# Attention first, then an ffn with seven of eight quarter products in both matmuls

## The chip, the cores and the metric

The kernel runs on one core of one Trainium2 chip. The core has a matrix engine (TensorE, PE in the profile, with its weight loads as PEld), a vector engine (VectorE, DVE), an activation engine (ScalarE, ACT), GpSimd (POOL), a queue engine that issues most DMAs (SyncE, SP), an on-chip memory of 128 partitions (SBUF), and eight accumulator banks for the matrix engine's results (PSUM). The metric is device time in microseconds (us), of which lower is better. All data is float32 unless said otherwise.

## The reference

Routed attention over 4 batches, 8 heads, 768 positions and head size 64, and on its output, as 3072 tokens of 512 features, a two-matmul ffn with 2048 hidden features.

```python
q_assign = argmax(q_n @ c_n.T)          # 16 centroids of each head; k_assign likewise
mask     = q_assign[..., :, None] == k_assign[..., None, :]
scores   = where(mask, (q @ k.T) / sqrt(D), -1e9)
attn     = exp(scores - max(scores));  attn /= sum(attn) + 1e-9
x        = (attn @ v).transpose(0, 2, 1, 3).reshape(3072, 512)
h        = x @ w_in                      # 512 x 2048
g        = h * erf(softplus(h))
out      = g @ w_out                     # 2048 x 512
```

The weights arrive as 64-bit floats and are turned into float32 on the chip.

## The kernel before, in words

**Attention.** Two heads of a batch form a pair; there are 16 pairs, four to a batch. `route` transposes q and k of a pair on DVE, multiplies them with the centroids on PE (`psim`), finds each position's best centroid, and writes it as extra rows of small bfloat16 tiles (`qm`, `km` in the trace). `shift` multiplies those tiles on PE (`sm`) and takes maxima on DVE (`nmx`), which give a shift for each query; `turn` transposes the shifts, and six row DMAs put them back into `qm`. A unit is one block of 128 keys against half of the queries (384) of a pair: `scores` makes four f32 matmuls' worth of `sc` and two bfloat16 ones, and ACT takes the exponential (`pr`). `accumulate` adds the exponentials on POOL (`acc`), `attend` multiplies them with v on PE (`av`), and after the sixth key block `divide` sums over partitions on PE (`psum`), forms the reciprocal on ACT and DVE, and writes the attention output to tiles `xT`, transposed, features on partitions. There are 12 units to a pair, 192 in all.

**Weights.** `fetch` brings a 512-wide piece of a weight as 64-bit words; `convert` turns it into float32 with three passes on ACT, two on DVE and one on POOL. There are 32 such steps.

**The ffn.** A chunk is `TB` = 256 tokens; there are 12. `hidden` makes, for each of the 16 blocks of 128 hidden features, four matmuls of 256 columns over the 512 input features, and DVE copies two blocks at a time from PSUM to `g`. `gate` runs softplus and erf on ACT and leaves the products with `h` to POOL. `project` makes, for each 128 tokens, 16 matmuls of 512 columns. For the last four chunks `project_fast` uses a form with seven products of quarter size in place of eight: its factors are sums of quarters of `g` and of `w_out`, made by DVE and POOL.

**Order.** The first four pairs (batch 0) run in "slots", one unit each: `plan` lists how many steps of `route` and `shift`, of this pair and of the next, and how many conversion steps go into each slot. The class `InOrder` pins every engine's instructions in the written order until `FIRST`. From then on attention of batches 1 to 3 goes two units at a time, and between the units a generator of ffn matmuls, `ffn_stream`, is drawn on by `pump` for as many cycles as keep the ffn in step. The ffn of batch 3 (three chunks) comes last and alone. So the ffn of a batch runs beside the attention of the next one.

A block of ffn work in the present form, the two lines that the change replaces:

```python
te.matmul(hp[:, a], lhsT=w_in[:, r, f0 : f0 + P], rhs=xTs[b * HP + r][c], ...)      # 768 of these
te.matmul(po, lhsT=gs[n][:, ft, tt * P : (tt + 1) * P], rhs=w_out[:, ft], ...)      # 8 chunks x 2 x 16
```

Nearly all instructions are recorded through line 61, the wrapper's call, so they are told apart by the names of their tiles.

Of the kernel before, what the change touches and what calls it, by code (L numbers as in the profile page):

```python
# [9 lines left out]
F32 = mybir.dt.float32  # L10
# [9 lines left out]
P = 128  # L20
# [11 lines left out]
GW = 2  # L32
TB = 256
NCHUNK = B * S // TB
# [3 lines left out]
OUT_AT = (4, 5, 6, 7, 4, 5, 6, 7, 5, 6, 7, 8, 7, 8, 8, 8)  # L38
# [5 lines left out]
XBUFS = (5, 6, 6)  # L44
SLOTS = 5


ASIDE = (*range(5), 6, *range(8, 8 + 2 * NJ), 10 + 2 * NJ, 12 + 2 * NJ)
REST = 4
FIRST = 2 * NJ * HP - 3  # L50
# [19 lines left out]
def kernel(  # L70
# [21 lines left out]
    stage = pool("stage", 1)  # L92
    vp = pool("vp", 2)
    rowp = pool("rowp", 2)
    routep = pool("routep", 1)
    small = pool("small", 2)
    accp = pool("accp", 2)
    xTp = pool("xTp", 1)
    actp = pool("actp", 2)
    gp = pool("gp", 2)  # L100
    outp = pool("outp", 1)
    ps_s = pool("ps_s", 2, space=PSUM)
    ps_x = pool("ps_x", 4, space=PSUM)

# [3 lines left out]
    rank = const.tile([P, C], F32, name="rank")  # L108
# [3 lines left out]
    w_in = const.tile([P, DM // P, DFF], F32, name="w_in")  # L112
    w_out = const.tile([P, NFT, DM], F32, name="w_out")
# [77 lines left out]
    n_w_in = len(w_steps)  # L191
    for f in range(NFT):
        w_steps.append((w_out[:, f], moe_w_out[f * P : (f + 1) * P]))


    places = [n % 8 for n in range(n_w_in)] + list(OUT_AT)
    converted = [0]

    def half_tile():
        return actp.tile([P, NFT // 2, TB], F32, name="a_s")  # L200

    steps = {}
    cut = []

    def fetch(done):

        for n in range(max(done + 1, 0), min(done + 5, len(w_steps))):
            at = places[n]
            if n in steps or (at < 8 and at in places[done + 1 : n]) or (at == 8 and n > done + 2):
                continue  # L210
            t = half_tile() if at == 8 else w_out[:, 2 * at : 2 * (at + 1)]
            t = t.rearrange("p f t -> p (f t)")[:, 0 : 2 * LC]
            nc.sync.dma_start(out=t.bitcast(U32), in_=w_steps[n][1])
            words = t.rearrange("p (n w) -> p n w", w=2)
            steps[n] = words[:, :, 1], words[:, :, 0], t.bitcast(I16)[:, 1 : 4 * LC : 4]

    def split(upto):

        for n in range(len(cut), upto + 1):
            if n not in steps:  # L220
                return
            cut.append(n)
            hi, lo, _ = steps[n]
            ae.activation(out=w_steps[n][0], in_=hi, func=ACT.Abs, scale=UP)
            ae.activation(out=lo.bitcast(I32), in_=lo.bitcast(U32), func=ACT.Copy, scale=2.0**-29)

    def signs(n):

        hi, _, upper = steps[n]

        ae.activation(out=upper, in_=hi, func=ACT.Prelu, scale=2.0**-25, alpha=2.0**90)

    def convert():

        for n in range(len(w_steps)):
            split(n)
            _, lo, _ = steps[n]
            w = w_steps[n][0]
            ve.tensor_scalar(out=w, in0=w, scalar1=2.0, scalar2=None, op0=ALU.max)
            signs(n)  # L240
            split(n + 1)

            fetch(n - 2 if n < n_w_in else n - 1)
            yield
            ve.tensor_scalar(
                out=w.bitcast(U32), in0=w.bitcast(U32), scalar1=3, scalar2=None, op0=ALU.logical_shift_left
            )

            ge.tensor_tensor(out=w.bitcast(I32), in0=w.bitcast(I32), in1=lo.bitcast(I32), op=ALU.add)
            converted[0] = n + 1  # L250
            yield

    load_qk(0)
    fetch(-1)
# [39 lines left out]
    def route(p):  # L294
# [37 lines left out]
        yield from (choose if p <= HP else choose_later)(p, sim, mx, hot, hotT, low, vectors)  # L332

    def choose(p, sim, mx, hot, hotT, low, vectors):
# [35 lines left out]
    def choose_later(p, sim, mx, hot, hotT, low, vectors):  # L370
        n = HW // C
        ve.tensor_tensor(
            out=sim, in0=sim, in1=mx.unsqueeze(2).to_broadcast([P, n, C]), op=ALU.is_equal
        )
        yield
        vectors("k")
        yield

        ve.tensor_tensor(
            out=sim, in0=sim, in1=rank.unsqueeze(1).to_broadcast([P, n, C]), op=ALU.mult  # L380
        )
        ve.reduce_max(out=mx, in_=sim, axis=AX.X)

        for r, op in ((slice(0, D), ALU.is_equal), (slice(D, P), ALU.subtract)):
            ve.tensor_tensor(
                out=hot[r].rearrange("p (g c) -> p g c", c=C), in0=sim[r],
                in1=mx[r].unsqueeze(2).to_broadcast([D, n, C]), op=op,
            )
        ve.transpose(out=hotT, in_=hot)
        yield  # L390
        for half in range(2):
            cols = slice(half * HW, (half + 1) * HW)
            for e in range(2):
                r = slice(e * D, e * D + Q)
                g = slice(half * Q, (half + 1) * Q)
                ve.tensor_scalar_mul(out=low["q"][r, e, cols], in0=hotT[g], scalar1=own[g, e : e + 1])
                g = slice(D + half * Q, D + (half + 1) * Q)
                ae.copy(out=low["k"][r, e, cols], in_=hotT[g])
        yield

    def shift(p):
# [5 lines left out]
        for h in range(2):  # L409
# [17 lines left out]
            if p >= HP:  # L427
                yield
                turn(p, h)
# [32 lines left out]
    xTs = {}  # L462
    done = set()
# [33 lines left out]
    def accumulate(u):  # L497
# [4 lines left out]
        if j == 1:  # L502
            st["acc", half] = accp.tile([P, 2, HW], F32, name="acc")
# [18 lines left out]
    def divide(u):  # L522
# [22 lines left out]
        x = xTs.setdefault(p, {})  # L545
        lo = half * HW
        while lo < (half + 1) * HW:
            c = lo // TB
            hi = min((c + 1) * TB, (half + 1) * HW)
            if c not in x:  # L550
                x[c] = xTp.tile([P, TB], F32, name=f"xT{c}", bufs=XBUFS[c])
            mine = slice(lo - half * HW, hi - half * HW)
            ve.scalar_tensor_tensor(
                out=x[c][:, lo - c * TB : hi - c * TB], in0=av[:, mine], scalar=av[:, HW : HW + 1],
                in1=den[:, mine], op0=ALU.add, op1=ALU.mult,
            )
            lo = hi
        done.add((p, half))
# [5 lines left out]
    TJ = TB // P  # L564
    CPB = S // TB

    def gate(n):

        h = gs[n]
        half = NFT // 2  # L570
        s = [half_tile() for _ in range(2)]
        for i in range(2):
            ae.activation(out=s[i], in_=h[:, i * half : (i + 1) * half], func=ACT.Softplus)
        for i in range(2):
            ae.activation(out=s[i], in_=s[i], func=ACT.Erf)

        for i in range(0, NFT, GW):
            gating.append(
                functools.partial(
                    (ge if n < NCHUNK - 1 else ve).tensor_tensor, out=h[:, i : i + GW],  # L580
                    in0=s[i // half][:, i % half : i % half + GW], in1=h[:, i : i + GW], op=ALU.mult,
                )
            )
        resting[0] = REST
        if not spread[0]:
            gate_products()

    gating = []
    spread = [True]

    def gate_products(n=NFT):
        for product in gating[:n]:
            product()
        del gating[:n]

    gs = {}
    resting = [0]

    def hidden(n):
        b, c = n // CPB, n % CPB  # L600
        gs[n] = gp.tile([P, NFT, TB], F32, name="g")
        for fp in range(NFT // GW):
            while converted[0] < DM // P * (fp * GW * P // LC + 1):
                yield None
            hp = ps_x.tile([P, GW, TB], F32, name="hp", tag="x")
            for a in range(GW):
                f0 = (fp * GW + a) * P
                for r in range(HP):
                    te.matmul(
                        hp[:, a], lhsT=w_in[:, r, f0 : f0 + P],  # L610
                        rhs=xTs[b * HP + r][c],
                        start=(r == 0), stop=(r == HP - 1),
                    )
                    if (a, r) != (GW - 1, HP - 1):
                        yield 4 * TB
            ve.tensor_copy(out=gs[n][:, fp * GW : (fp + 1) * GW], in_=hp)
            if fp == NFT // GW - 1:
                gate(n)
            yield 4 * TB

    out_v = out.rearrange("(b j p) m -> b j p m", p=P, j=NJ)

    def project(n):
        b, c = n // CPB, n % CPB
        gate_products()
        for tt in range(TJ):
            po = ps_x.tile([P, DM], F32, name="po", tag="x")
            for ft in range(NFT):
                while converted[0] < n_w_in + ft + 1:
                    yield None  # L630
# [322 lines left out]
```

## Time and profile before

| what | value |
|---|---|
| time, median of 3 runs | 1193.4 us (1189.37 to 1197.01) |
| span of the profiled execution | 1195.2 us, mean granted clock 0.977 |
| PE busy | 1145.7 us, 5104 instructions |
| DVE, ACT, POOL busy | 567.2, 587.1, 470.0 us |
| `hp` matmul instructions (hidden) | 1536 of 256 columns |
| `po` matmul instructions (projection) | 512 of 512 columns |
| seven-product projections | 448 instructions of 256 columns |
| gate products on POOL | 88 of 512 elements, 1317 ns each |
| table loads on ACT | 110 of 1283 ns |

Each f32 matmul of the program shows as two instructions in the profile. The busy time of PE is a modelled time: instructions overlap, so the time from one instruction's start to the next is more telling than the mean length of one. The page has the span in 40 slices of 29.9 us with busy shares in tenths; the windows of the trace give the same for stages of one's choice.

### The profile page before, as it was taken

How to read it: one execution, taken by the hardware profiler on the slowest of the kernel's cores; microseconds unless marked ns; L12 is line 12 of the kernel's file. 1: busy time of each engine (PE TensorE's matmuls, PEld its weight loads, DVE VectorE, ACT ScalarE, POOL GpSimd, SP SyncE). 2: the span in 40 equal slices, each digit the busy share in tenths (PEclk: the TensorE clock that was granted, in tenths of full speed). 3: DMA queues.
4: the chain of work that ended last, by engine and by line, in shares of the span. 5: the costliest groups of instructions: out<-in, count | busy, mean ns of one | idle time of the engine just before them, and what ended most of it. 6: DMA issues, size and time to landing. Idle time of an engine off the chain costs nothing.

```text
span 1195.2 us, 13871 instructions
## 1 busy us (share of the span) xinstructions
PE 1145.7 (96%) x5104; PEld 660.6 (55%) x5104; DVE 567.2 (47%) x1061; ACT 587.1 (49%) x682; POOL 470.0 (39%) x472
## 2 busy tenths in 40 slices
PE   4999979899999989999999999999999999999998
PEld 1333356563544545465465455556457456888887
DVE  7788785435443444344263345334345215442351
ACT  5789896764334445172454354256254255404220
POOL 3677774545333434154344244225244336213000
PEclk8899989899999899999999998999999999999999
DMA  7652443110202001020200201002000000000000
GB/s 137 164 128 41 93 151 60 60 26 24 36 14 36 23 7 34 9 46 4 36 22 1 49 10 27 22 9 40 1 23 10 9 9 1 1 18 1 18 9 27
DMA packets 141715, 42.97 MB, mean 36 GB/s; under 512 B 133456, under 2 KB 135504, under 8 KB 141648
## 3 DMA queue, kind: packets, MB, share of 16 engines
q1 hardware_dynamic: 138512, 41.70, 15.7%
q10 hardware_dynamic: 3136, 0.39, 0.3%
q8 instruction: 40, 0.66, 0.2%
q14 instruction: 27, 0.22, 0.1%
HBM read 35.68 MB, written 6.29 MB: 35 GB/s over the span
## 4 chain that ended last, share of the span: by engine, by line
PE 77%; ACT 8%; issue 7%; DVE 5%; DMA 2%; POOL 1%; SPq 0%; DVEq 0%; ACTq 0%
PE hp L61 25%; PE sc L61 21%; PE po L61 16%; PE av L61 8%; PE sm L61 4%; ACT km L61 2%; ACT L61 2%; DVE nmx L61 2%; ACT w_out L61 2%; PE psim L61 1%; PE psum L61 1%; ACT pr L61 1%; DMA in_q<-in_q_dram 1%; ACT inv L61 1%; DVE den L61 1%
## 5 line engine op out<-in xcount | busy, mean ns | idle before, releaser
L61 PE MATMUL hp<-xT,w_in 128*128 128x256 f32 x1536 | 385.4, 393 | 8.6 <-DVE xT L61 6.3
L61 PEld LDWEIGHTS hp<-xT,w_in 128*128 128x128 f32 x1536 | 292.9, 195 | 111.0 <-issue 60.8
L61 POOL TENSOR_TENSOR acc<-acc,pr 128x384 f32<-128x384 f32 x256 | 237.6, 959 | 281.9 <-ACT pr L61 281.8
L61 DVE TENSOR_REDUCE nmx<-sm 128x1 f32<-128x384 f32 x384 | 195.8, 550 | 146.7 <-PE sm L61 145.8
L61 PE MATMUL po<-w_out,g 128*128 128x512 f32 x512 | 250.1, 599 | 0.6 <-DVE den L61 0.6
L61 ACT ACT_TABLE_LOAD x110 | 141.1, 1283 | 201.3 <-DVE g L61 98.3
L61 ACT ACTIVATE pr<-sc 128x768 f32<-128x768 f32 x192 | 146.9, 806 | 147.8 <-PE sc L61 147.4
L61 PE MATMUL sc<-qT,kT 64*128 64x384 f32 x768 | 184.6, 534 | 4.8 <-ACT pr L61 4.7
L61 POOL TENSOR_TENSOR g<-a_s,g 128x512 f32<-128x512 f32 x88 | 113.2, 1317 | 182.6 <-ACT a_s L61 182.6
L61 PE MATMUL av<-pr,in_v 128*64 128x386 f32 x768 | 140.4, 497 | 0.0
L61 DVE COPY g<-hp 128x512 f32<-128x512 f32 x96 | 65.9, 687 | 148.9 <-PE hp L61 148.6
L61 PEld LDWEIGHTS po<-w_out,g 128*128 128x128 f32 x512 | 93.3, 190 | 66.5 <-issue 56.5
L61 PE MATMUL sm<-km,qm 128*128 128x384 bf16 x384 | 103.5, 338 | 16.4 <-DVE nmx L61 6.8
L61 PEld LDWEIGHTS sc<-qT,kT 64*128 64x128 f32 x768 | 70.9, 190 | 83.0 <-issue 47.0
L61 POOL TENSOR_TENSOR acc<-pr,pr 128x384 f32<-128x384 f32 x64 | 65.4, 1042 | 93.3 <-ACT pr L61 93.3
L61 PEld LDWEIGHTS av<-pr,in_v 128*64 128x64 f32 x768 | 49.3, 136 | 80.2 <-issue 69.6
L61 PEld LDWEIGHTS <-qm 128*128 128x128 bf16 x384 | 34.8, 99 | 84.3 <-issue 69.6
L61 DVE SCALAR_TENSOR_TENSOR den<-psum,inv 128x384 f32<-128x384 f32 x32 | 17.8, 557 | 128.3 <-ACT inv L61 127.9
L61 ACT ACTIVATE w_out<-w_out 128x512 int32<-128x512 uint32 (+2 forms) x68 | 62.0, 956 | 2.8 <-DMA w_out<-in_moe_w_out_dram 2.3
L61 ACT ACTIVATE a_s<-g 128x2048 f32<-128x2048 f32 x24 | 45.9, 1910 | 34.1 <-DVE g L61 34.0
L61 PE MATMUL sc<-qm,km 64*128 64x384 bf16 x384 | 60.5, 330 | 0.5 <-DMA qm<-nmT 0.5
L61 ACT COPY nmT<-pn 6x128 bf16<-6x128 bf16 x31 | 7.7, 249 | 97.3 <-PE pn L61 95.3
(112 smaller groups left out, 854.4 us busy)
## 6 DMA issues: line engine op xcount, KB each, us to landing
w_out<-in_moe_w_in_dram SPq DMA_DIRECT2D x16, 512.0 KB, 6.0
in_q<-in_q_dram SPq DMA_DIRECT2D x64, 96.0 KB, 3.1
in_v<-in_v_dram SPq DMA_DIRECT2D x32, 192.0 KB, 3.0
w_out<-in_moe_w_out_dram SPq DMA_DIRECT2D x12, 512.0 KB, 3.6
in_k<-in_k_dram SPq DMA_DIRECT2D x60, 96.0 KB, 3.3
out_dram<-osb SPq DMA_DIRECT2D x16, 256.0 KB, 2.0
qm<-nmT SPq DMA_DIRECT2D x186, 0.2 KB, 1.7
a_s<-in_moe_w_out_dram SPq DMA_DIRECT2D x4, 512.0 KB, 3.5
```

The lines of the kernel that those rows point to most:

```text
L61: ins = getattr(self.engine, name)(*args, **kw)
```

## The change

The mixed stage goes. All 16 pairs of attention run in pinned slots as batch 0 did; the output of each half pair is stored to a scratch tensor in device memory, `x_dram`. Then the ffn runs alone, also in pinned order, in six chunks of `CT` = 512 tokens, read back by `load_x`. Both of its products use the seven-product form: for a 2 x 2 grid of quarters on each side, four sums on the left and four on the right are made beforehand (`left_forms`, `right_forms`), and seven products take the place of eight. Its purpose is to do the ffn with fewer matmul instructions.

```diff
-TB = 256
-NCHUNK = B * S // TB
+CT = 512
+NCHUNK = B * S // CT
+HT, HK, HF, HM = CT // 2, DM // P // 2, NFT // 2, DM // 2
+FG = HF // 2
...
+QUIET = (0, 3, 5, 6, 7, 9, 10, 11)
...
+    more_in = const.tile([P, 3, HK, DFF // 2], F32, name="more_in")
+    more_out = const.tile([P, 3, HF, HM], F32, name="more_out")
+    x_more = const.tile([P, 3, HK, HT], F32, name="x_more")
+    x_dram = dram.tile([DM, B * S], F32, name="x_dram")
...
+        nc.sync.dma_start(
+            out=x_dram[r * P : (r + 1) * P, b * S + half * HW : b * S + (half + 1) * HW], in_=x
+        )
...
+    def left_forms(engine, a11, a12, a21, a22, new):
...
+            functools.partial(plus_of, new[0], a21, a22, engine),
+            functools.partial(minus_of, new[1], new[0], a11, engine),
+            functools.partial(minus_of, a21, a11, a21, engine),
+            functools.partial(minus_of, new[2], a12, new[1], engine),
...
+    ORDER = (1, 2, 6, 7, 5, 3, 4)
...
+    def bank():
+        n_banks[0] += 1
+        if n_banks[0] % 3:
+            return ps_x.tile([P, 512], F32, name="wx", tag="x")[:, 0:HT]
+        return ps_s.tile([P, 2, 512], F32, name="ws", tag="s")[:, 0, 0:HT]
+
+    def block(pieces, c11, c12, c21, c22, done=lambda i: None, lot=1):
+        after = {
+            1: [lambda m: ae.copy(out=c12, in_=m)],
+            2: [lambda m: plus_of(c11, m, c12)],
+            6: [lambda m: plus_of(c12, m, c12)],
+            7: [lambda m: plus_of(c21, m, c12)],
+            5: [lambda m: plus_of(c12, m, c12), lambda m: plus_of(c22, m, c21)],
+            3: [lambda m: plus_of(c12, m, c12)],
+            4: [lambda m: minus_of(c21, c21, m)],
+        }
+        for i in ORDER:
+            m = bank()
+            pairs_of = pieces(i)
+            for k, (lhsT, rhs) in enumerate(pairs_of):
+                te.matmul(m, lhsT=lhsT, rhs=rhs, start=(k == 0), stop=(k == len(pairs_of) - 1))
+            for f in after[i]:
+                f(m)
+            done(i)
+            for work in aside_work[:lot]:
+                work()
+            del aside_work[:lot]
```

`hidden(n, lot)` runs four blocks, each of seven products of two matmuls, for half of the hidden features; `project(n, s)` runs one block of seven products of eight matmuls, for half of the chunk's tokens, with `lot=4`. Work that need not be on the path (gate curves, gate products, sums of `g`, of `x` and of `w_in`) goes into the list `aside_work`, from which `block` takes `lot` pieces after each product; the curves and their products stand `GATE_LAG` = 6 pieces apart. The gate products, on POOL before, are on DVE now; POOL makes the sums of `w_out`. Accumulation from PSUM is on DVE, and the first product of a block is copied by ACT. The banks for the products come from both PSUM pools, six in turn.

In the attention part, conversion steps are spread over all pairs: `convert` has four parts to a step, and the slots in `QUIET` take one part each, two steps to a pair where batch 0 took four. All pairs use `choose`, the form of the one-hot product that batch 0 used, and `choose_later` is gone. The tiles for the attention output and the sums of exponentials are fixed places in `more_out`, and the weights are staged in `more_in`, both of which the ffn's sums fill later.

## The prediction

> **What bounds the kernel now.** I first read the engine totals and the clock line of the page, then busy time by stage, and then, inside the stages, the chain that ended last and single groups.
>
> ```profile
> PE 1145.7 (96%) x5104; PEld 660.6 (55%) x5104; DVE 567.2 (47%) x1061; ACT 587.1 (49%) x682; POOL 470.0 (39%) x472
> PEclk8899989899999899999999998999999999999999
> ```
>
> TensorE is busy nearly always and no other engine reaches half. So first ask how many TensorE instructions there are, and how fast a stream of them runs. The stages (columns: start:end, us, then busy us and count of PE, PEld, DVE, ACT, POOL, then clock, DMA share, GB/s):
>
> ```profile
> 62.00:94.00 32.00, 30.90 (x168) 10.07 (x166) 26.13 (x51) 27.39 (x40) 24.86 (x26) 1.00 0.47 103
> 94.00:125.00 31.00, 29.91 (x166) 9.72 (x164) 25.26 (x51) 27.36 (x40) 23.95 (x24) 1.00 0.29 50
> 125.00:240.00 115.00, 99.30 (x448) 59.22 (x443) 75.22 (x130) 93.69 (x113) 68.71 (x62) 0.90 0.34 92
> 240.00:1010.00 770.00, 760.30 (x3299) 409.77 (x3298) 324.24 (x596) 352.40 (x401) 295.24 (x294) 0.99 0.10 21
> 1060.00:1195.00 135.00, 130.81 (x605) 114.53 (x603) 40.74 (x73) 25.55 (x16) 9.87 (x8) 1.00 0.05 15
> ```
>
> The first two rows are the pinned attention of batch 0, one head pair each (12 slots), with weight conversion beside it: PE idles only 1.1 us per pair, but ACT is at 27.4 us of 31.5, and DVE at 25.7. The third row is the hand-over to the mixed stage: ACT 93.7 of 115, PE idle 15.7 us, clock 0.90. The fourth is attention mixed with ffn, the fifth is ffn alone. The chain of waits gives the rates (start, us, what):
>
> ```profile
> 122.26 1.01 PE sc L61 x6
> 123.27 0.80 PE av L61 x4
> ...
> 972.36 1.81 PE sc L61 x12
> ...
> 985.86 4.04 PE av L61 x24
> ...
> 1142.20 44.91 PE sc L61 x208
> ```
>
> The last row carries most of the forecast: in the seven-product projection that the kernel already has for its last four chunks, 208 f32 instructions of 256 columns take 44.91 us without a break, 215.9 ns each. The others show that an attention unit costs PE 1.01 + 0.80 = 1.81 us when the slots are pinned, and 0.91 + 0.67 = 1.58 us in the mixed stage, where units go in twos and the value products in groups of six.
>
> **What the Trainium skill says.** "TensorE: Matmul & The Clock Gate", section "Wait — 56ns, not 53.3ns?", gives 215.7 ns between warm matmuls of 512 columns. An f32 instruction of 256 columns here takes the same 215.9, so I treat it as 512 columns of streaming, with weight loads hidden; the trace agrees (PEld 114.5 of 135 us beside it). Its section "What's actually happening" says the clock halves after an idle window of about 3.4 us and returns after a busy one; the trace agrees: from 150 to 160 us PE is busy 3.75 us and the clock is 0.60, and by 170 it is 1.00. "VectorE: DVE Perf Modes", section "The perf-mode tier table", has f32 additions of two tensors at one element per cycle only; the trace has 0.62 us for 512 elements (four gate products in 2.49 us, from 1149.46) and 0.42 for 256 with one input in PSUM (the group of the fast projection's sums). So DVE work has a firm price.
>
> **The change, part by part.** Each f32 matmul of the program is two instructions in the profile.
>
> (1) Hidden product. Before: 12 chunks x 16 blocks x 4 = 768 matmuls, 1536 instructions of 256 columns, 331.6 us at 215.9 ns. After: 6 chunks x 8 blocks x 7 products x 2 = 672 matmuls, 1344 instructions, 290.2 us. Saved: 41.4.
>
> (2) Output product. Before: 512 instructions of 512 columns at 1.72/4 = 0.43 us (the mixed stage's groups of four), 220.2 us, and 448 of 256 columns, 96.7. After: 12 half chunks x 7 x 8 = 672 matmuls, 1344 instructions, 290.2 us. Saved: 26.7. The new ffn is 2688 instructions, 580.3 us.
>
> (3) Attention pinned for all 16 pairs. The last 12 pairs lose the mixed stage's cheaper order: 12 x (1.81 - 1.58) = 2.8 us a pair, plus maxima products at 0.215 instead of about 0.17 us, 24 x 0.045 = 1.1, and some idle time: 30.3 against some 26 (12 x 1.58 + 24 x 0.17 + 3 for sums, similarities and the one-hot products). Against this the conversion is spread over all 16 pairs: two weight steps a pair instead of four. A step costs ACT 0.71 + 0.68 + 1.35 = 2.7 us, DVE 1.1, POOL 1.3. So per pair ACT falls from 27.4 to 22.0, DVE from 25.7 to 23.5, POOL from 24.4 to 21.8. PE's own 30.3 us a pair stays. Bounds for a pair: 31.4 us (mean distance of the pairs' similarity products, 62.65, 94.41 and 125.51, as if relief did nothing) and 28.5 (half way to the mixed rate). I take 30.6, PE's busy time and 0.3 idle. The extra scratch store per half pair (192 KB) is 6.3 MB in 500 us, beside a DMA share of 0.3 to 0.5 that falls with the slower weight fetches. It waits on DVE in the SP queue; behind it stand the six row stores of the shift maxima and the next loads. They have at least three slots (5 us and more), and the fetches wait there for POOL (about 2 us); I cost both at nothing, with 33 us a pair as the upper end.
>
> (4) DVE beside the ffn. Per block of seven products DVE has 7 accumulations from PSUM (two after product 5, none after product 1, which ACT copies), 60 x 7 x 0.42 = 176 us; gate products move from POOL to DVE, 96 x 0.62 = 60; sums of the hidden tile 96 x 0.62 = 60; x and w_in forms 40 x 0.62 = 25. In all 321 of 580 us. Locally: a hidden product lasts 4 x 0.216 = 0.86 us on PE; with one piece of extra work after it DVE needs 0.42 + 0.62 = 1.04, so DVE falls back 0.18 us per product, and six banks (5.2 us) take that up over the 8 products of a call that have such work. In the output product 3.45 us of PE stand against at most 0.42 + 4 x 0.62 = 2.9 of DVE.
>
> (5) The gate's curves, two table loads and two passes: 2 x 1.28 + 2 x 1.91 = 6.4 us on ACT, twice per half. Behind them waits ACT's copy of a block's first product, and behind that the whole chain of that block on DVE. In the output product the next such copy is 24 us off, so it costs nothing. In the first chunk the curves run beside hidden products with a copy every 6 us, and the first use of forms made only just before adds to it: a guess of 6 us, between 0 and 12.
>
> (6) Hand-over. The last unit's exponentials are followed by two POOL additions (1.9 us) and the sum product (0.8) before the ffn's first instruction on PE: 3 us. The eight forms (5 us of DVE) lie beside it, since products 1 and 2 need none. With the tail as now (3.5 us from the last matmul):
>
> 62.7 (pair 2's similarity product, as now) + 14 x 30.6 = 491.1; the last pair without work for a next one, 11 slots of 2.05, gives 513.6; + 3 = 516.6; + 580.3 = 1096.9; + 6 + 3.5 = 1106. A second way: -68 for (1) and (2); 12 x (30.6 - 26) = +55 for (3); and of the losses from 125 us on (1070 less 649 of ffn and 13 x 26 of attention, 83 us) some 70 go, as the hand-over with its low clock and waits on conversion is gone: 1195 - 83 = 1112.
>
> **The rivals.**
> A, DVE paces the ffn: if chained accumulations through one tile cost more than 0.42, all 336 hidden products run at 1.04 us: +59, 1165. For it: every DVE accumulation now feeds the next. Against: the present fast projection chains its sums too, 0.75 us for two (1158.42).
> B, slower: if PE waits for a bank at every other product and for ACT's copy, 672 x 0.15 = 101 us, 1207, and more if such gaps lower the clock. For it: product groups are 4 instructions short. Against: six banks, and DVE is needed 55% of the time.
> C, attention alone runs at 33 us a pair, held by the SP queue or by shift maxima: +34, 1140. For it: waits of PE on maxima and casts stand on the chain in the pinned stage. Against: at four weight steps they cost only 1.1 us a pair.
> D, ACT was the true bound of the pinned slots: 28.5 a pair, 1077. Against: PE is busy 96% there.
>
> **How the numbers follow.** Forecast 0.58, A 0.10, B 0.06, C 0.15, D 0.11. The range, 1078 to 1146, takes in the forecast with its own spread (30.0 to 31.4 a pair, 0 to 12 for the first chunk), C, and nearly D; A and B stay out. Faster by over 1% holds in all but B and a milder B: 0.92; same 0.03; slower 0.05.
>
> **What would show it.** Similarity products 30 to 31.4 us apart in all 15 pairs; ffn from about 515 us, in the chain as rows of PE at 0.216 us an instruction; clock 1.00 after 40 us; DVE 55% busy in the ffn. Wrong: PE under 97% busy after 550 us with waits on DVE or ACT (A, B); pairs over 32 us, waiting on row stores (C).

## The result, and the profile after

The changed kernel takes 1137.38 us (median of four runs, 1137.32 to 1137.58), against 1191.38 us for the kernel before (four runs, 1187.77 to 1197.01): a ratio of 0.955, 95% interval 0.952 to 0.959. The direction was right and the time lies in the range, but the gain is 54 us where 87 were forecast (1193.4 - 1106). The page's engine totals and clock line show a matrix engine that is no less busy than before, but whose busy time is 68 us shorter, as much as the two product counts were said to save (41.4 + 26.7). That the two agree so closely is partly luck, since busy time also holds the clock (a mean of 0.977 before, 0.991 now) and the order of attention:

```profile
PE 1077.4 (95%) x5318; PEld 670.2 (59%) x5318; DVE 697.2 (61%) x1380; ACT 554.6 (49%) x703; POOL 373.4 (33%) x394
...
PEclk8999999999999999998999999999999999999999
```

So the counts don't explain the missing 30 us. The windows by stage do (start:end, length, busy us and count of PE, PEld, DVE, ACT, POOL, clock, DMA share, GB/s). The first two rows are one head pair each, from similarity product to similarity product, as in the view of before. Then come the last pair, the hand-over, the ffn's first stretch, and the rest of the ffn.

```profile
61.24:92.91 31.67, 30.05 (x166) 9.75 (x165) 23.70 (x45) 23.49 (x34) 21.25 (x24) 1.00 0.39 84
92.91:124.59 31.68, 30.06 (x167) 9.72 (x165) 23.72 (x45) 23.51 (x34) 21.25 (x24) 1.00 0.42 84
474.54:520.00 45.46, 43.84 (x243) 14.38 (x241) 27.41 (x51) 32.58 (x47) 33.76 (x37) 1.00 0.08 22
520.00:534.40 14.40, 11.10 (x53) 3.47 (x51) 9.59 (x10) 5.95 (x8) 13.97 (x13) 0.88 0.04 15
534.40:620.00 85.60, 74.37 (x318) 61.44 (x318) 56.58 (x111) 30.77 (x30) 22.21 (x16) 0.96 0.05 15
620.00:1132.10 512.10, 512.02 (x2373) 450.40 (x2371) 253.21 (x541) 145.62 (x128) 0.00 (x0) 1.00 0.05 19
```

Three readings. In a pair, ACT fell from 27.4 us to 23.5, DVE from about 25.7 to 23.7 and POOL from about 24.4 to 21.3, and still a pair lasts 31.67 us, not less than the 31.68 and 31.11 of before (similarity products at 62.65, 94.33 and 125.44): PE waits 1.6 us of each, where it waited 1.1. In the ffn's first 86 us PE idles 11.2 us, at a mean clock of 0.96. From 620 us on PE is busy 512.02 of 512.10 us; that is the forecast's ffn, 0.216 us an instruction.

The span in the forecast's own terms (1106 forecast, 1135.6 in the profiled run):

| milestone | forecast, us | trace, us | adds to the miss |
|---|---|---|---|
| start of the last pair (14 pairs after the similarity product of pair 2) | 491.1 | 506.2 (61.24 at first, 474.54 at the last product, one pair on) | +15.1 |
| last exponential of attention | 513.6 | 527.2 | -1.5 |
| first ffn matmul | 516.6 | 534.36 | +4.2 |
| ffn: 580.3 for the count, 6 for the first chunk | 586.3 | 597.7, to 1132.1 | +11.4 |
| tail | 3.5 | 3.5 | 0 |

Two places, then: the pairs, and the ten or so waits around the start of the ffn.

### The profile page after: what moved, and what is told of

The parts are those of the page before. It is cut to its first block, busy times and chain, and to the rows that moved or that the text cites. A ratio compares the mean times of both kernels' runs of the same rounds, so it can differ in the third digit from the quotient of the medians.

```text
span 1135.6 us, 14931 instructions
## 1 busy us (share of the span) xinstructions
PE 1077.4 (95%) x5318; PEld 670.2 (59%) x5318; DVE 697.2 (61%) x1380; ACT 554.6 (49%) x703; POOL 373.4 (33%) x394
## 4 chain that ended last, share of the span: by engine, by line
PE 76%; ACT 9%; DVE 7%; DMA 4%; issue 2%; SPq 1%; POOL 0%; DVEq 0%; ACTq 0%
PE wx L57 32%; PE ws L57 16%; PE sc L57 12%; PE av L57 8%; PE sm L57 5%; ACT km L57 4%; DVE nmx L57 3%; DMA in_k<-in_k_dram 2%; ACT pr L57 2%; PE psum L57 1%; DVE g L57 1%; PE psim L57 1%; ACT a_s L57 1%; ACT L57 1%; SPq L149 1%
## 5 line engine op out<-in xcount | busy, mean ns | idle before, releaser
L57 POOL TENSOR_TENSOR more_out<-more_out,pr 128x384 f32<-128x384 f32 x256 | 237.0, 953 | 42.1 <-ACT pr L57 40.6
L57 PE MATMUL sm<-km,qm 128*128 128x384 bf16 x384 | 100.0, 335 | 20.7 <-DVE nmx L57 15.1
L57 DVE TENSOR_TENSOR g<-wx,g 128x256 f32<-128x256 f32 x192 | 78.0, 420 | 51.7 <-PE wx L57 46.2
L57 PE MATMUL wx<-x_own,w_in 128*128 128x256 f32 x384 | 97.9, 385 | 1.3 <-DVE w_in L57 1.1
L57 DVE TENSOR_TENSOR g<-a_s,g 128x512 f32<-128x512 f32 x96 | 62.1, 684 | 45.6 <-ACT a_s L57 45.6
L57 PE MATMUL wx<-w_out,g 128*128 128x256 f32 x384 | 86.1, 379 | 0.0
L57 PEld LDWEIGHTS wx<-x_own,w_in 128*128 128x128 f32 x384 | 73.8, 193 | 13.5 <-DVE w_in L57 1.5
L57 PEld LDWEIGHTS wx<-w_out,g 128*128 128x128 f32 x384 | 73.0, 190 | 9.9
L57 POOL TENSOR_TENSOR more_out<-pr,pr 128x384 f32<-128x384 f32 x64 | 67.1, 1070 | 20.4 <-ACT pr L57 20.4
L57 PE MATMUL wx<-x_more,more_in 128*128 128x256 f32 x256 | 67.0, 385 | 6.7 <-DVE x_more L57 4.1
L57 ACT ACTIVATE more_in<-more_in 128x512 int32<-128x512 uint32 x64 | 64.5, 1007 | 0.7
```

Of the source, the lines that this page charges most:

```text
L57: ins = getattr(self.engine, name)(*args, **kw)
```

## The experiments

**The pairs.** Where is the 1.6 us? PE's groups of the changed kernel between 61 and 475 us, 13 pairs (busy us, mean ns, then idle time before them and what ended it):

```profile
L57 PE MATMUL av<-pr,in_v 128*64 128x386 f32 x624 | 134.9, 511 | 5.2 <-DVE nmx L57 5.2
L57 PE MATMUL sm<-km,qm 128*128 128x384 bf16 x312 | 79.4, 329 | 16.1 <-DVE nmx L57 12.6 <-ACT km L57 3.5
```

21.3 us in all, over half of it before `sm`, the product for the shift maxima, with the maxima `nmx` on DVE as what ended it. An operation that waits for a maximum does so for its PSUM bank, since `nmx` is no input of `sm`. PE's timeline inside one pair shows the shape (start, us, then the instruction and idle time before it):

```profile
201.45 0.66 PE L57 MATMUL sm<-km,qm 128*128 128x384 bf16 x3
202.44 0.32 PE L57 MATMUL sm<-km,qm 128*128 128x384 bf16 x1 [0.32 <-DVE nmx L57]
202.69 0.87 PE L57 MATMUL av<-pr,in_v 128*64 128x386 f32 x4
```

Three products go out and the fourth waits 0.32 us; the same at 205.49 and 213.37. The plan puts two `shift` steps (four products) in a row in three slots of a pair; the pool of banks has four, and the value accumulator `av` holds one. The same pattern stands in the kernel before:

```profile
107.53 0.32 PE L61 MATMUL sm<-km,qm 128*128 128x384 bf16 x1 [0.32 <-DVE nmx L61]
```

Two theories: "banks" (the order of PE, whatever the load) and "conversion" (DVE and ACT are late because conversion is in their queues). Two kernels tell them apart. The first takes all conversion out of the slots and does it after attention:

```diff
-QUIET = (0, 3, 5, 6, 7, 9, 10, 11)
+QUIET = ()
```

> All 32 conversion steps stand after the attention instead of two per pair. Theory 'banks' (maxima products wait for DVE to free one of the three PSUM banks left to them, whatever the conversion does): the similarity products of two pairs stay 31.2 to 31.7 us apart. Theory 'conversion' (the conversion's passes on ACT, DVE and POOL hold up the pinned slots): they come to 30.6 us or less. The whole is longer under both, by about 32 x 2.7 = 86 us of ACT passes after the attention, less what the attention gains.

Measured: 1216.48 us in a single run, since 32 steps now stand alone between attention and ffn. The pairs are what counts: 31.85 us apart, with no conversion at all. PE's groups in the same window:

```profile
L57 PE MATMUL av<-pr,in_v 128*64 128x386 f32 x624 | 134.9, 511 | 8.5 <-DVE nmx L57 8.5
L57 PE MATMUL sm<-km,qm 128*128 128x384 bf16 x312 | 79.4, 329 | 14.8 <-DVE nmx L57 12.6 <-ACT km L57 2.2
```

The 12.6 us before `sm` are the same to the tenth, the wait for `km` fell from 3.5 to 2.2, and the wait before `av` grew from 5.2 to 8.5. The conversion theory falls for the larger part, the wait for maxima. The second kernel leaves conversion alone and moves one of the two `shift` steps in each of those slots behind the value products:

```diff
+SPLIT = (6, 7, 10)
...
-            advance(p + 1, behind)
+            advance(p + 1, min(behind, 1) if r in SPLIT else behind)
...
+        if r in SPLIT:
+            advance(p + 1, behind - min(behind, 1))
```

> In the slots 6, 7 and 10 of a pair, the second of two maxima steps (two products each) moves behind the value products. Theory 'banks': the waits of 0.32 us before the fourth maxima product go, three a pair, about 1 us: pairs come 30.7 us apart, and 15 pairs give 14 us: 1123 us. Theory 'conversion': the order of PE matters nothing, pairs stay at 31.7, 1137 us within 3.

Measured: 1126.73 us, ratio 0.947 (0.944 to 0.950) against the kernel before, 10.7 us under the changed kernel; pairs 30.93 us apart, so 14 x 0.75 = 10.5 us. That is a little short of the expectation. (In the profiled run the ffn starts 12.4 us earlier, at 521.92, but lasts 2.8 us longer, in part because of the clock: see the last section.) PE's group and a stretch of its timeline:

```profile
L58 PE MATMUL sm<-km,qm 128*128 128x384 bf16 x316 | 80.9, 330 | 7.9 <-DVE nmx L58 4.2 <-ACT km L58 3.7
```

```profile
196.44 0.50 PE L58 MATMUL sm<-km,qm 128*128 128x384 bf16 x2
196.86 0.87 PE L58 MATMUL av<-pr,in_v 128*64 128x386 f32 x4
197.67 0.50 PE L58 MATMUL sm<-km,qm 128*128 128x384 bf16 x2
198.09 0.92 PE L58 MATMUL sc<-qT,kT 64*128 64x384 f32 x4
```

Two products, value products, two products: the wait for a bank falls from 12.6 to 4.2 us. What remains is at another place of the same kind, and 5.7 us before `av` that this edit doesn't touch. "Banks" is shown for the waits of the fourth product.

The wait before `av` is new: before, `av` follows the sums' product without a stop.

```profile
98.13 0.87 PE L61 MATMUL av<-pr,in_v 128*64 128x386 f32 x4
```

On DVE the one-hot comparison `hot`, which stands just ahead of the maxima that `av` waits for (it takes a new bank of the same pool there), has become slower. Here it is in the kernel before, the changed kernel and the one without conversion in the slots:

```profile
96.46 0.56 DVE L61 TENSOR_TENSOR hot<-sims,mx 128x384 bf16<-128x384 f32 x1
63.36 1.05 DVE L57 TENSOR_TENSOR hot<-sims,mx 128x384 bf16<-128x384 f32 x1
63.77 1.30 DVE L57 TENSOR_TENSOR hot<-sims,mx 128x384 bf16<-128x384 f32 x1
```

In the kernel before, POOL is idle then (95.74 to 99.21), because a conversion step that is not ready stands ahead of its next additions of exponentials. With that step out of slot 2 the additions come earlier and run beside `hot`. The wait before `av` follows the length of `hot`, pair for pair: none at 0.56 us, 0.06 at 0.72 (in the kernel with slot 2 below), 0.40 at 1.05, 0.65 at 1.30. So taking the conversion step out of that slot itself cost about 0.4 us a pair. No run moves the additions alone; that a DVE operation with both operands in on-chip memory is slower beside POOL is seen again at the start of the ffn.

Does conversion cost nothing, then? One more part per pair, in slot 2, is tried by itself, since a kernel below (`forms`) contains it:

```diff
-QUIET = (0, 3, 5, 6, 7, 9, 10, 11)
+QUIET = (0, 2, 3, 5, 6, 7, 9, 10, 11)
```

> The changed kernel with a ninth conversion part a pair, in slot 2, nothing else; the conversion ends two pairs earlier. Theory 'place': pairs 32.5 to 33 us apart wherever a sign pass (1.35 us of ACT) comes before the casts, with waits of PE on casts of over 1 us; 1145 to 1150 us. Theory 'banks' alone: pairs as now, 1136 to 1139 us.

Measured: 1142.86 us, ratio 0.961 (0.957 to 0.965), 5.5 us over the changed kernel and somewhat under the expectation; pairs 31.7 to 32.9 us apart. PE's group, same window:

```profile
L57 PE MATMUL sm<-km,qm 128*128 128x384 bf16 x304 | 77.4, 329 | 26.4 <-ACT km L57 14.1 <-DVE nmx L57 12.3
```

The bank wait is unchanged (12.3), and a new one has come: 14.1 us for `km`, the casts and one-hot rows that ACT writes, where it was 3.5. Removing all conversion gained nothing and adding one part to one slot cost 5 us. Place and amount can be told apart within this run: every pair has nine parts, but which of them fall just ahead of the one-hot rows changes from pair to pair. In the pairs from 95.41 and 224.96, where ACT has 0.67 us of conversion there, a pair takes 31.7 us; in the others, with 1.3 to 2.0 us, 32.4 to 32.9. So it is the ACT passes right ahead of those rows that count, not the number of parts.

**Counting the two halves of the change.** A kernel with attention first and the same pinned ffn, but eight plain quarter products in place of seven, each output accumulated in PSUM, without the sums:

```diff
-    ORDER = (1, 2, 6, 7, 5, 3, 4)
+    ORDER = (((1, 1), (2, 2)), ((1, 7), (2, 3)), ((7, 1), (4, 2)), ((7, 7), (4, 3)))
...
-            for f in after[i]:
-                f(m)
+            (ve.tensor_copy if i else ae.copy)(out=(c11, c12, c21, c22)[i], in_=m)
```

> The ffn as in the changed kernel, but with eight quarter products accumulated in PSUM and no sums of factors. Theory 'count' (PE bounds the ffn at 0.216 us an instruction): 3072 instructions instead of 2688, +83 us, less some 10 to 15 us of stalls in the first chunk that the sums cause: 1205 to 1212 us, so that attention first, by itself, is slower than the kernel before. Rival (the sums and accumulations on DVE cost the ffn about what seven products save): 1160 us or less.

Measured: 1201.98 us, ratio 1.010 (1.007 to 1.013), under the expectation, since 18 us of stalls (below) go with the sums and not 10 to 15. Its ffn in one window:

```profile
532.60:1197.00 664.40, 664.17 (x3073) 584.20 (x3072) 136.37 (x279) 176.53 (x158) 0.00 (x0) 1.00 0.05 16
```

PE doesn't stop in 664 us. This kernel has 64 ffn instructions' worth more than the kernel before, whose last four chunks already used seven products for the output: in instructions of 256 columns 1536 + 1536 against 1536 + 1024 + 448, or by the forecast's own terms 663 us against 649. Of its 12.6 us more (1201.98 against 1189.37, the kernel before in the same group of runs) that is 14.7. So moving attention ahead, by itself, is worth about nothing (2 us faster, less than the interval): what the hand-over to the mixed stage had cost is about what the mixed stage's cheaper order had saved. Seven products then bring 64.6 us (1201.98 - 1137.38). Their count is worth 384 instructions x 0.2159 = 82.9; the other 18 us are lost where the sums begin, and this kernel, which has no sums, doesn't lose them. That is the 17.4 us by which the ffn of the changed kernel is longer than its count.

**The start of the ffn.** PE's timeline of the changed kernel from the last value product on (idle time in brackets):

```profile
531.62 2.81 PE L57 MATMUL psum<-more_out,minus 128*64 128x384 f32 x4 [3.30 <-POOL more_out L57]
...
540.60 1.13 PE L57 MATMUL wx<-x_more,more_in 128*128 128x256 f32 x4 [0.88 <-DVE den L57]
...
569.47 1.13 PE L57 MATMUL wx<-x_own,w_in 128*128 128x256 f32 x4 [1.12 <-DVE w_in L57]
...
592.68 1.13 PE L57 MATMUL wx<-x_more,w_in 128*128 128x256 f32 x4 [1.71 <-ACT g L57]
...
599.67 2.07 PE L57 MATMUL wx<-x_more,more_in 128*128 128x256 f32 x4 [4.13 <-DVE x_more L57]
```

Three causes: POOL's last additions before `psum` (four, behind its last conversion step, where the forecast had two), sums that come late (`den` behind eight of them, `w_in`, `x_more`), and the first copy of a block behind the gate's curves on ACT (`g`). After 3.30 us of idle, four `psum` instructions take 2.81 us instead of 0.87, and after 4.13 us four ffn ones take 2.07 instead of 1.03: the clock has halved. (`psum` takes more than twice as long because its second two also stand behind POOL's last addition, which ends at 532.84.) And the first sums are slow. DVE of the changed kernel at the hand-over, then POOL at the same time:

```profile
533.31 1.75 DVE L57 TENSOR_TENSOR x_more<-x_own 128x512 f32<-128x512 f32 x1
535.09 1.64 DVE L57 TENSOR_TENSOR x_more<-x_own,x_more 128x512 f32<-128x512 f32 x1
...
543.22 0.41 DVE L57 TENSOR_TENSOR g<-wx,g 128x256 f32<-128x256 f32 x1
```

```profile
532.80 1.71 POOL L57 TENSOR_TENSOR more_out<-w_out 128x512 f32<-128x512 f32 x1
534.59 1.59 POOL L57 TENSOR_TENSOR more_out<-w_out,more_out 128x512 f32<-128x512 f32 x1
```

Both engines start a sum every 1.6 to 1.8 us, in step, while the DVE sum with an input in PSUM (the row of `g`) takes its 0.41. To see whether POOL's `w_out` sums are the cause, one kernel holds them back until the first chunk's hidden product is done:

```diff
+    last = g_of[0, 1, 1][:, 1, FG - 1, HT - 1 : HT]
+    ge.tensor_tensor(out=more_out[:, 0, 0, 0:1], in0=last, in1=last, op=ALU.add)
     for f in range(0, HF, 2):
         for work in right_forms(ge, *w_out_parts(f, 2)):
```

> POOL's sixteen sums of w_out start only after the first chunk's last hidden block. Theory 'contention' (DVE's sums of two SBUF tiles run 1.4 to 1.75 us because POOL works beside them): the eight sums at the hand-over fall to 0.62 to 0.75 us each, and the losses of PE in the first 20 us of the ffn shrink by 3 to 8 us, but DVE's gate products and sums in the next hidden call get slower instead. Rival (these sums are slow of themselves, by their strides): they stay at 1.4 us and more. Time 1130 to 1142 us under the first, 1137 under the second.

Measured: 1140.26 us in a single run. Two of the same sums on DVE, and PE's longest wait:

```profile
532.47 0.68 DVE L57 TENSOR_TENSOR x_more<-x_own 128x512 f32<-128x512 f32 x1
533.18 0.69 DVE L57 TENSOR_TENSOR x_more<-x_own,x_more 128x512 f32<-128x512 f32 x1
```

```profile
599.50 2.08 PE L57 MATMUL wx<-x_more,more_in 128*128 128x256 f32 x4 [10.09 <-DVE x_more L57]
```

The sums take 0.68 us with POOL idle, so their slowness is POOL's doing. But the time didn't fall: POOL's sums now run beside the gate products and the sums of the next chunk's `x`. The latter take 1.65 to 1.76 us each there, and the wait for them grew from 4.13 to 10.09 us. The cost moved.

Three kernels then took the causes one by one. `forms` does the first sums in the last pair's slots, where PE is the bound, POOL's later, and two of the four `x` sums for the second chunk earlier. To be done with `w_in` in time it converts nine parts a pair:

```diff
+        if p + 1 == NPAIR:
+            if not early:
+                prepare(4 * len(w_steps))
+                early += right_forms(ve, *x_parts(0))
+                for f in range(0, HF, 2):
+                    early += left_forms(ve, *w_in_parts(f, 2))
+            early.pop(0)()
```

> The sums of x and w_in that the first chunk needs are spread over the last pair's twelve slots and the first hidden call; the conversion ends a pair earlier (nine parts a pair); the first two sums of the second chunk's x come before the last two products of the call before; POOL's sums of w_out start one call later. Theory 'sums' (the first chunk's loss beyond the forecast is PE waiting for sums on DVE that run at 1.4 us beside POOL): waits of PE on sums, 2.5 us up to 550, 2.6 up to 572 and 4.1 at 599, go, and the cold clock after the last; 1126 to 1129 us. Rival (the gate's curves on ACT and their products hold DVE, sums or not): the waits move and the time stays within 1134 to 1140.

Measured: 1135.59 us, ratio 0.956 (0.954 to 0.959), no gain, and the expectation missed. The waits at the start of the ffn did fall, but with the ninth part most pairs take 32.4 to 33.1 us, as in the run with slot 2 alone, above.

`curves` moves the first copy of each block, in the first chunk and the call after it, from ACT to DVE, and sets the curves and their products nine pieces apart there instead of six:

```diff
-            1: [lambda m: ae.copy(out=c12, in_=m)],
+            1: [lambda m: (ve.tensor_copy if by_dve[0] else ae.copy)(out=c12, in_=m)],
```

> In the first chunk and the call after it, the first product of a block is copied by DVE and not by ACT, and curves and their products stand nine pieces apart, not six. Theory 'curves' (in the first chunk ACT's copies queue behind 6.4 us of curves): the waits of PE on ACT copies (1.71 at 592, 0.31 at 617) and some of the 4.1 us at 599 go, 1131 to 1135 us. Theory 'sums': 1135 to 1138.

Measured: 1136.55 us, ratio 0.957 (0.954 to 0.960), no gain. PE's waits on ACT's copies are gone, and its timeline has instead, where 4.13 stood:

```profile
599.82 1.90 PE L57 MATMUL wx<-x_more,more_in 128*128 128x256 f32 x4 [5.11 <-DVE x_more L57]
```

PE's idle time in the ffn did fall, from 11.2 to 9.0 us, but the mean clock of its first 86 us fell too, from 0.96 to 0.91.

`forms2` is `forms` with eight parts a pair as in the changed kernel; the place of the weights' staging is shifted so that ten of the first twenty sums fit in the last pair, the rest beside the first hidden product:

```diff
-        t = places[:, n % PLACES]
+        t = places[:, (n + 4) % PLACES]
...
+            if r == 0:
+                ops = [left_forms(ve, *w_in_parts(f, 2)) for f in range(0, HF, 2)]
+                early += right_forms(ve, *x_parts(0)) + ops[0][:3] + ops[1][:3]
+                later = [ops[0][3], ops[1][3]] + ops[2] + ops[3]
```

> The sums as in forms, but with the conversion left as in the changed kernel (eight parts a pair): staging places are turned by four, so that only the fourth sum of w_in must wait for the last steps, and ten sums of x and w_in lie in the last pair. Theory 'place' (in forms the ninth conversion part, an ACT pass ahead of the casts that the maxima products need, cost about 1 us a pair and ate the gain): pairs stay at 31.7 us and the ffn starts where it does now; 1126 to 1130 us. Rival (the sums never cost more than they cost elsewhere): 1134 to 1138 us.

Measured: 1130.25 us, ratio 0.951 (0.948 to 0.954), 7.1 us under the changed kernel, pairs at 31.68. Of its waits the largest left is now ACT's copy behind the curves:

```profile
604.08 1.03 PE L57 MATMUL wx<-x_own,more_in 128*128 128x256 f32 x4
607.86 2.06 PE L57 MATMUL wx<-x_more,w_in 128*128 128x256 f32 x4 [2.75 <-ACT g L57]
```

**Together.** Two kernels join the three edits: `best` with `forms`, `best2` with `forms2`; each also with `split_sm` and `curves`.

> The edits of split_sm, forms and curves together. If the three causes are separate their gains add: 1137.4 less 10.7, 9 and 3, 1112 to 1117 us, 0.937 of the kernel before. If pairs and first chunk share a cause (DVE), less: above 1120.

Measured: 1120.64 us, ratio 0.944 (0.941 to 0.946), short of the expectation for the same reason as `forms`: pairs at up to 32.9 us.

> The edits of split_sm, forms2 and curves together. Theory 'place': pairs 30.9 us apart, the ffn within 3 us of 580 from its start: 1108 to 1113 us. Rival: as best, 1118 to 1122 us.

Measured: 1110.4 us (1109.07 to 1113.92), ratio 0.934 (0.932 to 0.937): the best of all, 27.0 us under the changed kernel. Alone the edits gave 10.7, 7.1 and 0.8, together 18.6; joined they give 8 more. In the profiled runs that surplus lies in the ffn. Part of it is waits that had stood behind one another (PE's idle time in the ffn falls to 0.9 us, where the single edits would add up to some 4), but more of it is the clock: in the ffn's first 86 us its mean is 0.96 in the changed kernel, 0.93 and 0.91 with `split_sm` and `curves` alone, 0.98 with `forms2`, and 1.00 here. The start of its ffn, and the waits that PE has left from the last pair on:

```profile
520.00:606.00 86.00, 84.48 (x387) 73.04 (x388) 65.45 (x138) 32.92 (x23) 24.57 (x19) 1.00 0.05 15
```

```profile
520.65 1.68 PE L58 MATMUL psum<-more_out,minus 128*64 128x384 f32 x4 [2.62 <-POOL more_out L58]
...
574.33 1.13 PE L58 MATMUL ws<-x_own,w_in 128*128 128x256 f32 x4 [0.87 <-DVE x_own L58]
```

In 86 us at the start of the ffn, where the changed kernel idled 11.2, this one idles 1.5 (0.65 of it still before `psum`), at clock 1.00; pairs are 30.92 us apart, and the ffn starts at 522.26.

## Why the prediction was half right

**Right.** Steps (1) and (2), the product counts at 215.9 ns: the steady ffn runs at that rate, 2373 instructions in 512.1 us. Step (4) in the steady ffn: DVE keeps up with seven products (253 of 512 us busy, 49%, where 55% was forecast), and PE's 512.02 of 512.10 refutes rivals A and B there (B's sum was off besides: it has 672 waits, and the ffn has 336 + 84 = 420 products). The second way's terms for moving attention, +55 and -70, come to -15, where `eight` shows -2. The tail is as forecast. In a pair PE's own work is 30.05 us, forecast 30.3.

**Wrong, step (3): the idle time in a pair.** The step took a pair as "PE's busy time and 0.3 idle", 30.6 us, arguing from the halved conversion that ACT, DVE and POOL would be relieved. They were relieved almost as said (23.5, 23.7, 21.3 us, where ACT was to come to 22.0), and the idle time rose from 1.1 to 1.6 us. The term was mis-sized by 1.1 to 1.3 us, fourteen times over: 15 of the 30 us. The reading that failed is the one of before's 1.1 us: I took PE's idle time there as a result of the neighbours' load, and didn't look at what it stood in front of. The timeline of before already had three such waits of a fourth product, 0.27 to 0.32 us each, and `split_sm` shows that these are worth 0.75 us a pair, while `conv_late` shows that the conversion's load is worth nothing to them. And relief had a cost that the step put at nothing: with the conversion step gone from slot 2, POOL's additions moved beside `hot`, 0.4 us a pair, some 5.6 of the 15 us. The upper bound of that step, "as if relief did nothing", was nearly the answer (31.4 against 31.7). Rival C named the holder, shift maxima, and was set aside because they cost only 1.1 us a pair; they did hold the pairs, at 31.8 us and not at 33. Its other holder, row stores in a queue, shows on PE with no more than 0.6 us in 13 pairs.

**Wrong, steps (5) and (6): the size of the start.** The hand-over was put at 3 us and took 7.2, the first chunk at 6 and took 17.4. The mechanisms were named (sums used just after they are made, the copy behind the curves, POOL's two additions), and the sizes were not worked out. The eight sums that were "5 us of DVE" ran from 527.98 to 540.00, 12 us, because each was priced at 0.62 us from a moment when POOL was still. (The trace of before had the other case too: at 1101.45, while POOL ends a gate product, a sum of 768 elements takes 2.00 us, and its like at 1103.71 takes 0.94.) The Trainium skill has the reason, in "SBUF — State Buffer", section "SBUF: two separate sides": a DVE operation with two SBUF inputs and a GpSimd operation that reads SBUF exclude each other at a shared port, and the one that comes second waits for the whole of the other. The trace agrees: 1.24 to 1.75 us beside POOL, 0.68 without, and 0.41 as ever for a sum with one input in PSUM. In step (4) I had called the price firm. At the hand-over itself that is the smaller part: `eight`, without any sums, still waits 2.40 us there for POOL's last additions and starts its ffn 1.7 us earlier (532.67), so the forecast's 3 us for POOL and `psum` was short even without the sums: POOL has four additions to make there after its last conversion step, 3.6 us in `eight` and 4.9 beside DVE's sums, not two in 1.9. In the first chunk it is the place of the pieces that counts more: of 11.2 us idle, 2.5 stand behind the slow sums up to 550 us, 2.6 behind `w_in` sums that go one to a product (567 to 572 us, at 0.68 us each), 2.0 behind the curves, and 4.1 behind the four sums of the second chunk's `x`, which come all at once just before they are used. The other 6.2 us of the 17.4 are the lower clock after the waits (a mean of 0.96 over 86 us, so by estimate 3.4 us) and restarts. That the waits could be removed at all is shown by `best2`: with the bank order and the start mended, the same plan takes 1110 us, 4 over the forecast. So the forecast priced a schedule that the change could have had, and not the one it has. Both mis-sized terms lie outside the forecast's own spread (30.0 to 31.4 us a pair, 0 to 12 for the first chunk), which by its terms ended at 1106 + 14 x 0.8 + 6, some 1123 us; that the time lies in the range is owed to the room that was left for rival C.

Still open: whether the 0.4 us before `av`, half of the idle time that `split_sm` leaves in a pair, would go if POOL's additions stood elsewhere, and how much of `forms2`'s 7.1 us is due to POOL's later sums and how much to DVE's earlier ones; no run separates them.

## What to carry to other kernels

When a pinned order leaves the bounding engine idle, look at which instruction the idle time stands before and what resource it lacks, before giving the idle time to the load of a neighbour; moving one instruction tests it, emptying the neighbour's queue is the counter-test, read wait by wait, because it also moves what else that neighbour does. Before counting on relief, ask what the relieved engine will now do earlier, and beside what. Take the duration of an elementwise sum from a moment when the same neighbours are at work as in the new place. And where several waits stand one behind another at a change of stage, mend them together: singly they gave 1 to 7 us here, and joined with the bank order 27.

## What the hardware showed that was not expected

DVE and POOL sums of 512 elements with all operands in SBUF ran in step, one of each per 1.7 us; alone they take 0.68 and 1.27 us (POOL's from 549.41 in the changed kernel, where DVE has only sums with an input in PSUM, which neither slow POOL nor are slowed), so running them side by side saves 0.25 us of the 1.95 that they take in turn.

The clock halved after less idle time than I had thought it needs. The Trainium skill, in "TensorE: Matmul & The Clock Gate", section "What's actually happening", has an idle window of about 3.4 us; the traces here differ. In `forms2` PE ran warm until 605.1 us, idled 2.75 us, and the next four instructions took 2.06 us in place of 1.03. Nor need it be one wait. In `split_sm` two, with 1.1 us of work between them, were enough:

```profile
554.79 1.13 PE L58 MATMUL wx<-x_more,more_in 128*128 128x256 f32 x4 [1.18 <-DVE more_in L58]
557.04 2.08 PE L58 MATMUL wx<-x_own,w_in 128*128 128x256 f32 x4 [1.11 <-DVE w_in L58]
```

The same two waits of the changed kernel (the second is at 569.47 above) were not. In every trace here the clock changes only at whole multiples of 3.41 us from its other changes. Both waits of `split_sm` lie in one such stretch, 553.61 to 557.03, of which PE idles 2.3 us; those of the changed kernel fall into two, from 565.03 and from 568.44, with 1.3 us in each. Over all twelve traces, every stretch at full clock of which PE idled 59% or more was followed by one at half clock; between 33 and 56% it went both ways. So short waits on PE can cost more than their length, and how much depends on where they fall.
